# Two layers of recurrent-memory attention and linear attention: the last tile's key-value sum is masked from PSUM, and five of sixteen reciprocal products move from VectorE to GpSimd

## The chip, the cores and the metric

The kernel runs on one core of one Trainium2 chip. A core has five engines that work side by side, each with its own in-order queue: TensorE (PE, with its weight loads PEld), VectorE (DVE), ScalarE (ACT), GpSimd (POOL) and SyncE (SP, which only issues transfers here). The on-chip memory for operands is SBUF; matmul results land in PSUM, of which there are eight banks. The metric is the device time of one execution in microseconds (us); the figure for a kernel is the median of several executions.

## The reference, cut to what matters

Two blocks alternate, A, B, A, B, on a sequence of 2048 tokens of width 512, each with a layernorm in front and a residual sum behind.

Block A is attention with a recurrent memory. The tokens are cut into 64 segments of 32. Eight memory rows are put ahead of each segment, 32 heads of width 128 attend inside it, and the first eight output rows are the memory of the next segment. So segment s+1 can't start before segment s has given its memory.

Block B is linear attention with 32 heads of width 16:

```python
phi = lambda t: jnp.where(t > 0, t + 1, jnp.exp(t)) + 1e-06
kv = jnp.einsum('bhsd,bhse->bhde', pk, v)      # sum over all 2048 tokens
z = jnp.einsum('bhsd->bhd', pk)
num = jnp.einsum('bhqd,bhde->bhqe', pq, kv)
den = jnp.einsum('bhqd,bhd->bhq', pq, z)[..., None] + 1e-06
o = num / den                                   # then o @ wo
```

The sums kv and z run over every token. No output row of B can be made before the last tile of tokens has added its part. Both times that block B runs, this is a point that all work must pass.

## The kernel before, in words

Tokens are handled in 16 tiles of 128 rows. Block A runs as 64 steps, four to a tile. Block B is cut in three. `b_in` takes tile t as soon as block A has finished it: layernorm, keys, values and queries by matmul (lines 1247 and 1281), phi of the keys and queries (`phi`, lines 1231 to 1234), and then the tile's part of kv and z by matmul into two PSUM tiles (lines 1259 and 1265). The parts are added up in SBUF in fp32, `kva` by line 1274 and `za` by line 1276. phi(q) is stored to a scratch in device memory, and so is x.

`b_mid` runs once per block B, after the last tile. Line 1295 masks `kva` to the heads' diagonal blocks and casts it to bf16. Line 1299, four times, makes the matrix `zf_sb` from `za`. Then, for each of four chunks of 128, one matmul (line 1303) multiplies the masked sum with the output weights `MB_sb`, and the product is copied back over the weights. The kernel's helper for copies (`evac`, lines 623 and 624 in the profile) lets the planner choose ScalarE or VectorE.

`b_out` then runs per tile: four matmuls with `zf_sb` give the denominators (line 1353), ScalarE makes their reciprocal as exp(-ln(.)) (lines 1356 and 1358), VectorE multiplies phi(q) by it (line 1359, the reciprocal product), four matmuls with the folded weights give the output rows (line 1361), and VectorE adds them to x (line 1364). In the first block B, `b_out` of tile 0 stands between the two A blocks and the others are spread over the second A block. In the second block B, the sixteen run one behind another at the very end of the kernel ("the last stage"), from data loaded into the space of `Wq_sb`, with the reciprocals in the space of `Wk_sb`, and each result goes out by a store on SP's queue.

The order on each engine is not written by hand. `_Prog.schedule` is a greedy planner that runs when the program is built: it gives every operation a cost (`c_act`, `c_dve`, `c_pe`), keeps a clock for each engine and the eight PSUM banks, and takes the ready operation with the best priority. A priority is the step times 13.5 plus an entry of the table `OFFSET`, found by the stage's name and by the operation's number within that stage; the more negative, the earlier. The whole program, all four blocks, is planned in one go, so each engine's queue is fixed before the run, and what is planned late depends on everything planned before it.

`keep_busy` adds dependency-free matmuls on TensorE, at the lowest priority of their step ("fillers", line 1385). The table `FILL` names the TensorE operation behind which a group of them may start, by stage and number; where that number is not a TensorE operation, the group is left out:

```python
FILL = (("outL", 7, 8), ("resL", 0, 24), ("biL", 5, 4), ("biL", 18, 8), ("biL", 27, 8), ("bm", 7, 21), ("boF", 9, 22),
        ("prepF", 5, 4))
```

Here `biL` is `b_in` of the last tile, `bm` is `b_mid`; the group behind `bm` exists only in the first block B. GpSimd does no arithmetic after the setup: its queue issues transfers of x, phi(q) and of the residual rows (line 639).

Of the kernel before, what the change touches and what calls it, by code (L numbers as in the profile page):

```python
# [9 lines left out]
ALU = mybir.AluOpType  # L10
# [78 lines left out]
    "outL": (-183.35, -223.20, -247.40, -365.15, -74.00, -380.60, -56.90, -223.50, -345.60, -38.20),  # L89
    "resL": (-280.85, -402.40),  # L90
    "biL": (-330.50, -308.55, -333.35, -91.15, -389.95, -228.15, -76.30, -32.45, -294.50, -121.05, -167.60,
        -377.75, -262.40, -270.20, -25.45, -14.60, -313.50, 59.95, -373.25, -319.65, -43.90, -426.45, -404.80,
        159.50, 90.55, -275.05, -114.60, -274.80, -0.20, -245.85, -186.45, -160.00),
    "bm": (-410.80, -480.25, -344.35, -394.70, -170.00, -356.70, -6.85, 40.95, -34.25, 28.70, -27.10, -86.70, 81.00),
    "boF": (-189.35, -384.50, -486.20, -152.40, -345.90, -400.30, -157.90, -333.20, -255.25, -380.60, -218.45),
    "bo": (-354.35, -361.60, -26.00, -195.25, -364.05, -132.50, 137.45, -348.35, -267.60, -258.70, -358.25),
    "ldL": (-68.35, -367.55),
# [5 lines left out]
def c_act(n, ptr=0, sb=0):  # L103
    return 0.17 + 0.833e-3 * n + 0.09 * ptr + 0.04 * sb


def c_dve(n, rate=1):
    return 0.155 + 1.044e-3 * n / rate
# [6 lines left out]
def c_pe(n_mm, n):  # L115
    return n_mm * max(0.0335, (n / 2.4 + 3.0) * 1e-3)
# [390 lines left out]
def _build_kernel(nc, A_x, A_mem0, A_Wq, A_Wk, A_Wv, A_Wo, A_seg_len, B_wqkv, B_wo, out):  # L507
# [7 lines left out]
    NT = S // 128  # L515
# [15 lines left out]
    def sb(name, shape, dt=BF16):  # L531
        return E(nc.sbuf_tensor(name, shape, dt))
# [18 lines left out]
    maskbd_sb = sb("maskbd_sb", [128, 128])  # L551
# [30 lines left out]
    qTl = av(2 * 1024).rearrange("p (r h j x) -> p r h j x", r=2, h=8, j=4)  # L582
    kTl = av(2 * 1024).rearrange("p (r b j g c) -> p r b j g c", r=2, b=2, j=4, g=4)
# [13 lines left out]
    MB_sb = av(4 * D).rearrange("p (c f) -> p c f", c=4)  # L597
    zf_sb = av(4 * 128).rearrange("p (c f) -> p c f", c=4)
    kva = av(512, F32)
    za = av(4, F32)  # L600
# [17 lines left out]
    add = P.add  # L618
# [40 lines left out]
    for i in range(4):  # L659
# [4 lines left out]
        writes=["wqkv"], dsem="dwqkv", after=[P.nodes[-1]], lat=5.0)  # L664
# [38 lines left out]
    for j in range(4):  # L703
# [10 lines left out]
        writes=["selz"])  # L714
# [4 lines left out]
    tl = P.tile()  # L719
    add("pe", lambda t, tl=tl: t.matmul(tl.f32()[:, 0:128], A8_sb[0:8, :], A8_sb[0:8, :], start=True, stop=True), 0.06,  # L720
        reads=XV, tiles=[tl])
    evac(maskbd_sb[:, :], lambda tl=tl: tl.f32()[:, 0:128], 128, tiles=[tl], writes=["maskbd"])
    tl = P.tile()

    def _m0(t, tl=tl):
        for c in range(4):
# [4 lines left out]
         writes=["memT0"])  # L731
# [497 lines left out]
    def phi(tl):  # L1229
# [4 lines left out]
        add("dve", lambda v: v.scalar_tensor_tensor(e_sb, tl.f32()[:, :], 0.0, e_sb, ALU.max, ALU.add), c_dve(512),  # L1234
            reads=["e"], tiles=[tl], writes=["e"])

    def b_in(step, t, last):

        P.at(step, "biL" if t == NT - 1 else "bi")
        tl = layernorm(t)  # L1240
# [13 lines left out]
        kv, z = P.tile(), P.tile()  # L1254
# [12 lines left out]
            return x  # L1267
        add("pe", mz, c_pe(4, 8), reads=["e", "one"], tiles=[z])
        zv = lambda: z.f32()[:, 0:32].rearrange("p (c x) -> p c x", x=8)[:, :, 0]
        if t == 0:  # L1270
            add("dve", lambda v: v.tensor_copy(kva, kv.f32()[:, :]), c_dve(512), tiles=[kv], writes=["kva"])
            add("dve", lambda v: v.tensor_copy(za, zv()), c_dve(4), tiles=[z], writes=["za"])
        else:
            add("dve", lambda v: v.tensor_tensor(kva, kva, kv.f32()[:, :], ALU.add), c_dve(512), reads=["kva"],
                tiles=[kv], writes=["kva"])
            add("dve", lambda v: v.tensor_tensor(za, za, zv(), ALU.add), c_dve(4), reads=["za"], tiles=[z], writes=["za"])
# [11 lines left out]
    def half(v, b):  # L1288
        return v[:, 4 * b:4 * b + 4, :, :].rearrange("p h j x -> p (h j x)")

    def b_mid(step, n):

        P.at(step, "bm")
        km, kk = half(qTl[:, 0], 1), ("qTl", 0, 1)
        add("dve", lambda v: v.tensor_tensor(km.rearrange("p (c x) -> p c x", c=4), kva.rearrange("p (c x) -> p c x", c=4),
                                             maskbd_sb[:, :].unsqueeze(1).to_broadcast([128, 4, 128]), ALU.mult), c_dve(512),
            reads=["kva", "maskbd"], writes=[kk])
        for c in range(4):
            add("dve", lambda v, c=c: v.tensor_scalar_mul(zf_sb[:, c, :], maskbd_sb[:, :], za[:, c:c + 1]), c_dve(128, 2),
                reads=["za", "maskbd"], writes=["zf"])  # L1300
        for c in range(4):
            tl = P.tile()
            add("pe", lambda pe, c=c, tl=tl: pe.matmul(tl.f32()[:, :], km[:, 128 * c:128 * c + 128], MB_sb[:, c, :],
                                                       start=True, stop=True),
                c_pe(1, 512), reads=[kk, ("MB", c)], tiles=[tl])
            evac(MB_sb[:, c, :], lambda tl=tl: tl.f32()[:, :], 512, tiles=[tl], writes=[("MB", c)])


# [22 lines left out]
    def b_out(step, t, last):  # L1331
# [3 lines left out]
        x, xk = x_sb[:, k, :], ("x", k)  # L1335
        e, ek, rb, rk = OWN if t else LEFT
        free = []
        if last:
            rb, rk = RE[:, t, :].bitcast(F32), [("RE", t)]
            free = P.res["Wk"][1]  # L1340
            if t < NT - 1:
                e, ek, x, xk = XE[:, 0, t, :], [("XE", 0, t)], XE[:, 1, t, :], ("XE", 1, t)
            else:
                e, ek = e_sb, ["e"]
# [5 lines left out]
        def md(pe):  # L1350
# [5 lines left out]
        add("act", lambda a: a.activation(rb, td.f32()[:, :], ACTF.Ln, bias=eps6_sb[:, 0:1]), c_act(512, 1),  # L1356
            reads=["eps6"], tiles=[td], writes=rk, after=free)
        add("act", lambda a: a.activation(rb, rb, ACTF.Exp, scale=-1.0), c_act(512, 0, 1), reads=rk, writes=rk)
        add("dve", lambda v: v.tensor_tensor(e, e, rb, ALU.mult), c_dve(512), reads=ek + rk, writes=ek)
        for c in range(4):  # L1360
            add("pe", lambda pe, c=c: pe.matmul(ty.f32()[:, :], e[:, 128 * c:128 * c + 128], MB_sb[:, c, :],
                                                start=(c == 0), stop=(c == 3)),
                c_pe(1, 512), reads=ek + [("MB", i) for i in range(4)], tiles=[ty])
        add("dve", lambda v: v.tensor_tensor(x, x, ty.f32()[:, :], ALU.add), c_dve(512), reads=[xk], writes=[xk],
            tiles=[ty])
# [34 lines left out]
    for t in range(NT):  # L1400
        b_out(2 * NSEG + 2 + t, t, True)
# [44 lines left out]
```

The softmax here doesn't subtract the row's maximum and nothing guards it: scores larger than these inputs give would overflow.

## Time and profile before

| what | value |
|---|---|
| median of 9 executions | 1763.24 us (1759.85 to 1767.76) |
| profiled execution, own time | 1763.24 us |
| its span in the profile | 1761.1 us, granted TensorE clock 0.996 of full speed on average |
| TensorE busy | 1680.3 us, 95% of the span |
| VectorE, ScalarE busy | 1133.5 us and 1130.0 us, 64% each |
| GpSimd busy | 329.1 us, 19% |

The span is what the profiler saw of one execution; the 2.1 us between it and that execution's own time lie around it. Busy shares are means over the whole kernel. The two places that the change touches are short, about 10 us where the first block B turns into the second block A (860 to 871 us of the span) and the last 35 us, and there other engines end the waits than in the long middle. A line of the timeline gives start, length, engine, source line, operation, output and inputs, and in brackets how long the engine stood idle before and for what.

### The profile page before, as it was taken

The page shows a single profiled execution, that of the slowest core. Times are in us where ns is not written, and L with a number is a line of the kernel's source. Part 1 is how long each engine was busy: PE and PEld are TensorE (multiplying, and loading weights), DVE is VectorE, ACT ScalarE, POOL GpSimd, SP SyncE. Part 2 cuts the span into 40 slices and gives each one's busy share as a digit, 9 for nine tenths or more (in the row PEclk, how much of TensorE's full clock was granted, in tenths as well). Part 3 has the DMA queues.
Part 4 walks back from the last instruction along what each step waited for, and adds up shares of the span by engine and source line. Part 5 has one row for each costly group of instructions (what it writes and reads, how often), then busy time and mean ns, then how long its engine had stood idle before and what let it go on. Part 6 is the DMA issues. An engine that isn't in the chain of part 4 may idle for free.

```text
span 1761.1 us, 101223 instructions
## 1 busy us (share of the span) xinstructions
PE 1680.3 (95%) x46099; PEld 1113.8 (63%) x46178; DVE 1133.5 (64%) x3960; ACT 1130.0 (64%) x3069; POOL 329.1 (19%) x660
## 2 busy tenths in 40 slices
PE   5999999999999999999999999999999999999997
PEld 2666666666666666666666666666666666666664
DVE  2566666666666666666566666676666676666656
ACT  3666666666666666666476666666666666666664
POOL 2012211111121112222101221112221112222020
PEclk9999999999999999999999999999999999999999
DMA  9222222222222222222012222222222222223314
GB/s 378 75 37 45 47 44 45 48 43 42 45 46 45 43 51 39 46 48 45 16 32 39 46 48 48 49 40 48 49 43 45 47 42 49 48 45 59 45 32 132
DMA packets 228541, 97.48 MB, mean 55 GB/s; under 512 B 207096, under 2 KB 222256, under 8 KB 226576
## 3 DMA queue, kind: packets, MB, share of 16 engines
q1 hardware_dynamic: 204784, 58.64, 18.3%
q0 software_dynamic: 21744, 19.78, 5.0%
q10 hardware_dynamic: 1584, 12.58, 1.7%
q8 instruction: 361, 5.91, 1.5%
q14 instruction: 68, 0.56, 0.1%
HBM read 29.63 MB, written 10.49 MB: 23 GB/s over the span
## 4 chain that ended last, share of the span: by engine, by line
PE 77%; DMA 10%; ACT 6%; DVE 5%; issue 2%; POOL 1%; ACTq 0%; DVEq 0%
PE pb L794 40%; PE pb L1085 13%; DMA arena_sb<-arena_sb 5%; PE pb L1051 4%; PE pb L816 4%; PE pb L1247 3%; DMA dx_sb<-y_sb 2%; DVE arena_sb L624 2%; PE pb L937 2%; PE pb L1281 2%; ACT arena_sb L623 2%; DMA Wk_sb<-in_A_Wk_dram 1%; PE pb L1110 1%; PE pb L970 1%; PE pb L765 1%
## 5 line engine op out<-in xcount | busy, mean ns | idle before, releaser
L623 ACT ACTIVATE arena_sb<-pb 128x512 bf16<-128x512 f32 (+6 forms) x1375 | 674.6, 509 | 301.0 <-PE pb L794 220.7
L639 POOL DMA_DIRECT2D dx_sb<-y_sb x504 | 256.6, 515 | 1098.3 <-DVE arena_sb L624 484.4
L794 PE MATMUL pb<-Wk_sb,arena_sb 128*32 128x512 bf16 x5120 | 345.7, 381 | 14.9 <-DVE arena_sb L624 6.4
L794 PE MATMUL pb<-Wv_sb,arena_sb 128*32 128x512 bf16 x5120 | 354.8, 379 | 0.7 <-issue 0.7
L794 PE MATMUL pb<-Wq_sb,arena_sb 128*32 128x512 bf16 x5120 | 340.8, 381 | 0.5 <-DMA Wq_sb<-in_A_Wq_dram 0.5
L1085 PE MATMUL pb<-Wo_sb,arena_sb 128*32 128x256 bf16 x10368 | 330.9, 274 | 9.9 <-DVE arena_sb L987 8.7
L1085 PEld LDWEIGHTS pb<-Wo_sb,arena_sb 128*32 128x32 bf16 x10368 | 266.5, 97 | 43.1 <-DVE arena_sb L987 20.2
L624 DVE CAST arena_sb<-pb 128x512 bf16<-128x512 f32 (+3 forms) x459 | 232.5, 519 | 84.4 <-PE pb L794 65.4
L624 DVE COPY arena_sb<-pb 128x512 bf16<-128x512 bf16 (+2 forms) x422 | 150.3, 364 | 166.7 <-PE pb L816 151.7
L624 DVE COPY arena_sb<-arena_sb 32x256 bf16<-32x256 bf16 (+2 forms) x960 | 202.2, 211 | 78.1 <-DMA arena_sb<-arena_sb 18.8
L794 PEld LDWEIGHTS pb<-Wk_sb,arena_sb 128*32 128x32 bf16 x5120 | 131.6, 97 | 119.8 <-DVE arena_sb L624 9.0
L794 PEld LDWEIGHTS pb<-Wq_sb,arena_sb 128*32 128x32 bf16 x5120 | 132.2, 97 | 116.6 <-issue 2.4
L623 ACT ACTIVATE outW_sb<-pb 128x128 fp32r<-128x128 f32 x288 | 79.8, 277 | 159.7 <-PE pb L1085 155.4
L794 PEld LDWEIGHTS pb<-Wv_sb,arena_sb 128*32 128x32 bf16 x5120 | 116.3, 95 | 47.3 <-issue 2.2
L816 PEld LDWEIGHTS pb<-id_sb,arena_sb 128*32 128x32 bf16 x6304 | 110.8, 97 | 53.8 <-DVE arena_sb L624 12.1
L954 ACT ACTIVATE arena_sb<-pb 128x192 bf16<-128x192 f32 (+1 forms) x256 | 81.5, 329 | 93.0 <-PE pb L943 47.8
L816 PE MATMUL pb<-id_sb,arena_sb 128*32 128x128 bf16 x6304 | 136.0, 220 | 0.1
L1121 DVE TENSOR_TENSOR y_sb<-pb,outW_sb 64x256 bf16<-64x256 f32 x158 | 65.8, 417 | 87.7 <-ACT outW_sb L623 85.0
L1051 PE MATMUL pb<-arena_sb 128*128 128x128 bf16 x1024 | 113.9, 220 | 5.4 <-DVE arena_sb L624 4.3
L964 DVE TENSOR_TENSOR arena_sb<-arena_sb 128x128 bf16<-128x128 bf16 x504 | 86.3, 220 | 16.4 <-ACT arena_sb L954 15.4
L1051 PEld LDWEIGHTS pb<-arena_sb 128*128 128x128 bf16 x1024 | 69.4, 97 | 40.9 <-issue 19.6
L987 DVE TENSOR_TENSOR arena_sb<-pb,arena_sb 128x128 bf16<-128x128 f32 x252 | 67.9, 285 | 26.8 <-ACT arena_sb L975 16.2
(125 smaller groups left out, 1976.8 us busy)
## 6 DMA issues: line engine op xcount, KB each, us to landing
arena_sb<-arena_sb SPq DMA_TRANSPOSE x356, 2.9
Wq_sb<-in_A_Wq_dram ACTq DMA_DIRECT2D x1, 4096.0 KB, 13.6
Wk_sb<-in_A_Wk_dram ACTq DMA_DIRECT2D x1, 4096.0 KB, 24.4
Wv_sb<-in_A_Wv_dram ACTq DMA_DIRECT2D x1, 4096.0 KB, 34.9
Wo_sb<-in_A_Wo_dram SPq DMA_DIRECT2D x4, 1024.0 KB, 11.7
xs_scratch<-x_sb POOLq DMA_DIRECT2D x32, 128.0 KB, 2.1
pq_scratch<-arena_sb POOLq DMA_DIRECT2D x32, 128.0 KB, 2.5
dx_sb<-y_sb POOLq DMA_DIRECT2D x252, 12.0 KB, 2.1
```

What stands on the lines that cost most here:

```text
L623: return e.activation(o() if callable(o) else o, i() if callable(i) else i, ACTF.Copy)
L624: return e.tensor_copy(o() if callable(o) else o, i() if callable(i) else i)
L639: add(eng, lambda e: e.dma_start(o, i), 0.55 if eng == "pool" else 0.4, reads=reads, writes=writes, dsem="%s%d" % (kind, k), lat=lat + (0. ...
L794: r = pe.matmul(tl.f32()[32 * j:32 * j + 32, 0:512], blk[:, c, :], W[:, c, o:o + 512], start=(c == 0), stop=(c == 3), tile_position=(0, 32 ...
L816: r = pe.transpose(tt.bf16()[32 * j:32 * j + 32, 128 * i:128 * i + 128], img[:, k, o:o + 32], id_sb[:, :], tile_position=(0, 32 * j))
L954: add("act", lambda a: a.activation(PQ[:, r2, b, 0:nq], tl.f32()[:, 0:nq], ACTF.Exp, scale=SCALE), c_act(nq), tiles=[tl], writes=[("PQ", r ...
L964: add("dve", lambda v, a=a, p_=p_, w_=w_: v.tensor_tensor(wide(Pm[:, k, a, :]), p_.unsqueeze(2).to_broadcast([128, 4, 4, 8]), w_, ALU.mult ...
L987: add("dve", lambda v: v.tensor_tensor(oTb[:, s % NO, 16 * b:16 * b + 16, 0:8], pv.f32()[:, 0:128].rearrange("p (n q) -> p n q", q=8), Rm[ ...
L1051: r = pe.matmul(o, vimg[:, r2, e], Pbx[:, hh, :, :], start=i == 0, stop=False, skip_group_check=True)
L1085: r = pe.matmul(tl.f32()[32 * j:32 * j + 32, 0:256], oT[:, 4 * hh + n, :], Wo_sb[:, 8 * n + hh, 256 * d:256 * d + 256], start=(hh == 0 and ...
L1121: add("dve", lambda v: v.tensor_tensor(y_sb[0:64, k, :], tl.f32()[0:64, 0:256], outW[64:128, w, :].bitcast(F32), ALU.add), c_dve(256), rea ...
L1247: add("pe", lambda pe, c=c: pe.matmul(dst.f32()[:, :], xlnT[:, c, :], wqkv_sb[:, c, o:o + D], start=(c == 0), stop=(c == 3)), c_pe(1, 512) ...
```

## The change

In `b_in` of the last tile, the part of kv is no longer added to `kva`; it stays in its PSUM tile. In `b_mid` there are two masked operands in place of one: the sum of tiles 0 to 14 from SBUF, and the last tile's part straight from PSUM, into a second buffer (the first half of `kTl[:, 1]`). The two are added by the matmul with the output weights, which accumulates two products for each chunk, so there are eight such matmuls in place of four. In the last stage, the reciprocal products of tiles 1, 4, 7, 10 and 13 are issued on GpSimd with a planned cost of 1.3 us.

The table `OFFSET` loses the entry of the removed addition in `biL` and gains entries for the new operations in `bm`. The numbers of the operations in both stages shift by that, and `FILL` is as it was.

```diff
     "biL": (-330.50, -308.55, -333.35, -91.15, -389.95, -228.15, -76.30, -32.45, -294.50, -121.05, -167.60,
-        -377.75, -262.40, -270.20, -25.45, -14.60, -313.50, 59.95, -373.25, -319.65, -43.90, -426.45, -404.80,
-        159.50, 90.55, -275.05, -114.60, -274.80, -0.20, -245.85, -186.45, -160.00),
-    "bm": (-410.80, -480.25, -344.35, -394.70, -170.00, -356.70, -6.85, 40.95, -34.25, 28.70, -27.10, -86.70, 81.00),
+        -377.75, -262.40, -270.20, -25.45, -14.60, -313.50, 59.95, -373.25, -319.65, -43.90, -426.45, 159.50,
+        90.55, -275.05, -114.60, -274.80, -0.20, -245.85, -186.45, -160.00),
+    "bm": (-450.00, -415.80, -480.25, -344.35, -394.70, -170.00, -356.70, -356.70, -6.85, 40.95, 40.95, -34.25,
+        28.70, 28.70, -27.10, -86.70, -86.70, 81.00),
...
+    kv_last = [None]
...
-        if t == 0:
+        if t == NT - 1:
+            kv_last[0] = kv
+            add("dve", lambda v: v.tensor_tensor(za, za, zv(), ALU.add), c_dve(4), reads=["za"], tiles=[z], writes=["za"])
+        elif t == 0:
...
-        km, kk = half(qTl[:, 0], 1), ("qTl", 0, 1)
-        add("dve", lambda v: v.tensor_tensor(km.rearrange("p (c x) -> p c x", c=4), kva.rearrange("p (c x) -> p c x", c=4),
-                                             maskbd_sb[:, :].unsqueeze(1).to_broadcast([128, 4, 128]), ALU.mult), c_dve(512),
-            reads=["kva", "maskbd"], writes=[kk])
+        masked = lambda v: v.rearrange("p (c x) -> p c x", c=4)
+        kv = kv_last[0]
+        parts = ((half(qTl[:, 0], 1), ("qTl", 0, 1), lambda: kva, ["kva"], []),
+                 (kTl[:, 1, 0].rearrange("p j g c -> p (j g c)"), ("kTl", 1, 0), lambda: kv.f32()[:, :], [], [kv]))
+        for km, kk, v_, rd, tls in parts:
+            add("dve", lambda v, km=km, v_=v_: v.tensor_tensor(
+                masked(km), masked(v_()), maskbd_sb[:, :].unsqueeze(1).to_broadcast([128, 4, 128]), ALU.mult), c_dve(512),
+                reads=rd + ["maskbd"], tiles=tls, writes=[kk])
...
-            add("pe", lambda pe, c=c, tl=tl: pe.matmul(tl.f32()[:, :], km[:, 128 * c:128 * c + 128], MB_sb[:, c, :],
-                                                       start=True, stop=True),
-                c_pe(1, 512), reads=[kk, ("MB", c)], tiles=[tl])
+            for i, (km, kk, *_) in enumerate(parts):
+                add("pe", lambda pe, c=c, tl=tl, i=i, km=km: pe.matmul(tl.f32()[:, :], km[:, 128 * c:128 * c + 128], MB_sb[:, c, :],
+                                                                       start=i == 0, stop=i == 1),
+                    c_pe(1, 512), reads=[kk, ("MB", c)], tiles=[tl])
...
-        add("dve", lambda v: v.tensor_tensor(e, e, rb, ALU.mult), c_dve(512), reads=ek + rk, writes=ek)
+        if last and t % 3 == 1:
+            add("pool", lambda g: g.tensor_tensor(e, e, rb, ALU.mult), 1.3, reads=ek + rk, writes=ek)
+        else:
+            add("dve", lambda v: v.tensor_tensor(e, e, rb, ALU.mult), c_dve(512), reads=ek + rk, writes=ek)
```

## The prediction, made before the changed kernel was run

> **What bounds the kernel now.** First the page: busy shares, then the chain that ended last.
>
> ```profile
> PE 1680.3 (95%) x46099; PEld 1113.8 (63%) x46178; DVE 1133.5 (64%) x3960; ACT 1130.0 (64%) x3069; POOL 329.1 (19%) x660
> ...
> PE 77%; DMA 10%; ACT 6%; DVE 5%; issue 2%; POOL 1%; ACTq 0%; DVEq 0%
> ```
>
> TensorE bounds the kernel as a whole, and none of its work in block A is touched. A gain can only come from the short places where another engine ends the waits. So next the timeline of the turn from the first block B to the second block A:
>
> ```profile
> 865.29 0.68 DVE L1274 TENSOR_TENSOR arena_sb<-arena_sb,pb 128x512 f32<-128x512 f32 x1
> ...
> 865.86 1.04 PE L1385 MATMUL pb<-Wv_sb,id_sb 128*128 128x256 bf16 x8
> ...
> 866.05 0.68 DVE L1295 TENSOR_TENSOR arena_sb<-arena_sb,maskbd_sb 128x512 bf16<-128x512 f32 x1
> 866.06 0.60 ACT L1231 ACTIVATE arena_sb<-pb 128x512 bf16<-128x512 f32 x1 [1.67 <-PE pb L1281]
> ...
> 866.79 0.60 PE L1303 MATMUL pb<-arena_sb 128*128 128x512 bf16 x2
> ...
> 867.22 1.08 ACT L623 ACTIVATE arena_sb<-pb 128x512 bf16<-128x512 f32 x2 [0.56 <-PE pb L1303]
> ```
>
> Addition, mask, first product with the weights, copy: a chain on VectorE, TensorE, ScalarE. TensorE fills its wait with eight fillers; ScalarE stands 0.56 us. The second block B has the same picture: addition 1734.18, mask 1734.94, product 1735.68, copy 1736.11.
>
> Last, the end of the kernel, as busy time by stretches (PE, PEld, DVE, ACT, POOL, each with its count; clock; DMA) and as timeline:
>
> ```profile
> 1744.00:1748.00 4.00, 4.00 (x31) 2.18 (x30) 4.00 (x8) 4.00 (x9) 0.00 (x0) 1.00 0.36 123
> 1748.00:1752.00 4.00, 3.84 (x22) 1.56 (x21) 4.00 (x8) 4.00 (x9) 0.00 (x0) 1.00 0.32 107
> 1752.00:1756.00 4.00, 3.35 (x14) 1.04 (x14) 4.00 (x8) 2.73 (x6) 0.00 (x0) 1.00 0.30 100
> ```
>
> ```profile
> 1752.75 0.68 DVE L1359 TENSOR_TENSOR Wq_sb<-Wq_sb,Wk_sb 128x512 bf16<-128x512 bf16 x1
> 1753.35 0.68 DVE L1364 TENSOR_TENSOR Wq_sb<-Wq_sb,pb 128x512 bf16<-128x512 bf16 x1
> 1753.47 1.26 ACT L1358 ACTIVATE Wk_sb<-Wk_sb 128x512 f32<-128x512 f32 x2
> ...
> 1757.09 1.04 PE L1361 MATMUL pb<-arena_sb 128*128 128x512 bf16 x4 [0.16 <-DVE arena_sb L1359]
> 1758.16 0.69 DVE L1364 TENSOR_TENSOR x_sb<-x_sb,pb 128x512 bf16<-128x512 bf16 x1
> ```
>
> VectorE is full and ends last; ScalarE is full until 1754.73 and close behind; GpSimd is empty. Products and additions start 0.60 us apart.
>
> **The change, part by part**, against the profiled execution: own time 1763.24 us, the median too; span 1761.1.
>
> *Addition out of the chain.* Once the last tile's kv is in PSUM, the mask can start where the addition stood, at 865.29. The fp32 row of line 1274 reads PSUM at 0.68 us, the mask's row is 0.68, so the new mask is taken at 0.68. It ends 0.76 us earlier, at 865.97. The product can start at 866.03, where TensorE, without the eight fillers (next paragraph), is just past the queries' matmuls. But each chunk needs two products: 0.22 us more (four of line 1361 take 0.87) before the copy. So the copy may start at 867.22 - 0.76 + 0.22 = 866.68, behind phi's exponential, which ends at 866.66. Gain 0.54 us, at each block B. VectorE is relieved too, so `zf_sb` and phi(q) are no later; the weights' copies of line 624 ended at 869.06, ahead of the first output product at 870.32. The other six matmuls (1.3 us) have room there: TensorE runs 2.3 us of fillers.
>
> *Mask of tiles 0 to 14.* 0.68 us more on VectorE, at the highest priority, ready when tile 14's addition ends (830.70 and 1692.21). At 830.61 the softmax product of line 1026 is queued behind, then the copies that feed line 1051. TensorE has 3.5 us of key and query matmuls there, ScalarE its copies: cost 0, with 0 to 0.6 us as ends. If that cover goes, the next segment's value products are late.
>
> *Fillers.* The list of `b_in` shrinks by one, so number 27 is the exponential of phi(q), no TensorE operation: eight fillers vanish in both blocks, 0.87 us each, at 865.86 and 1734.75. Nothing waits for them. Number 7 of `b_mid` is now the second product of the first chunk, so 21 fillers may start earlier. They ended at 870.34, just where the output product started; TensorE has 1.3 us of products more and 0.87 us of fillers less to do before. If the planner keeps all 21 ahead of the output product, the first gain of 0.54 is lost; ends 0 and 0.54, taken at 0, since the planner issues fillers singly and prefers the product once ready. The granted clock is 0.50 from 1728 to 1732 in the last block and 1.00 from 1736; the dropped fillers lie after the rise, and matmuls follow at once.
>
> *Five products on GpSimd.* VectorE's 32 operations at 0.60 us become 27, so 3.0 us less. ScalarE now sets the floor: its last exponential, 0.54 us earlier, ends at 1754.19; then 0.06 to the product, 0.68, 1.13 to the addition (from 1757.03 to 1758.16) and 0.69, so 1756.75 against 1758.85 now. Of these 2.10 us, 0.54 are the earlier start and 1.56 belong to GpSimd's help. What a product lasts on GpSimd isn't in the trace. The nearest rows:
>
> ```profile
> L678 POOL TENSOR_SCALAR_AFFINE_SELECT arena_sb<-arena_sb 128x160 bf16<-128x160 bf16 x2 | 0.9, 468 | 0.1
> ...
> L678 POOL TENSOR_SCALAR_AFFINE_SELECT id_sb<-id_sb 128x128 bf16<-128x128 bf16 x1 | 0.3, 317 | 0.1
> ```
>
> From 32 columns (214 ns, setup) to 128 (317) it is 1.1 ns an element, from 128 (406) to 160 (468) 1.9. For 512 columns that makes 0.74 to 1.15 us with one operand, and 1.83 us if a second operand doubles the steeper slope. I take 1.2. One comes every three tiles, 3.3 us, so the queue holds; its only transfer there, the store of phi(q) at 1737.05, is ahead of all five. A late product stalls TensorE in order, with tiles behind it: tile 13's, from about 1752.0, ends at 1753.3, and TensorE needs 0.87 us each for tiles 13 and 14 before 15's starts at 1755.0. So it just fits; at 1.83 it costs some 0.5 us.
>
> Unknown is also what GpSimd's arithmetic does to VectorE; no row shows both at work. Let w be VectorE's loss per moved product. Help is the smaller of 1.56 and 5 x (0.60 - w). Low end w = 0: VectorE's rows keep their 0.68 us while GpSimd issues transfers. High end: VectorE stands through it, 1.83. I take 0.4, near the low end because only issues were seen beside it: help 1.0 us, ends +1.56 and -6.2.
>
> Here the Trainium skill speaks against the change: "SBUF — State Buffer", section "SBUF: two separate sides", says that a VectorE operation with two SBUF inputs and a GpSimd operation that reads SBUF exclude each other for a whole instruction. Line 1359 has two such inputs, line 1364 only one. "GPSIMD Engine Reference", section 3.1, states about 2.6 cycles an element at 1.2 GHz, an estimated 1.1 us here; VectorE blocked for all of it gives 5 x (0.60 - 1.1), a loss of 2.5 us in place of the gain of 1.0. No row of this trace shows the lock.
>
> *The second A block is planned anew.* Everything behind tile 14's addition in the first block B is planned from other clocks and banks, 900 us of it. How uneven that stretch is, GpSimd's stores of x show, four steps apart:
>
> ```profile
> 1104.16 0.56 POOL L639 DMA_DIRECT2D xs_scratch<-x_sb  x1 [1.88 <-DVE x_sb L1162]
> 1155.44 0.56 POOL L639 DMA_DIRECT2D xs_scratch<-x_sb  x1 [1.88 <-DVE x_sb L1162]
> ...
> 1471.46 0.56 POOL L639 DMA_DIRECT2D xs_scratch<-x_sb  x1 [1.92 <-DVE x_sb L1162]
> 1525.42 0.56 POOL L639 DMA_DIRECT2D xs_scratch<-x_sb  x1 [2.86 <-DVE x_sb L1162]
> ```
>
> The like work takes 51.28 us and 53.96 us. The fourteen distances from 949.58 to 1683.53 have a mean of 52.43 and a scatter of 0.97, so 3.6 us over fourteen; part of it is the spread of executions. All at the best (51.24) would be 16.6 us less, all at the worst 21.4 more. I take 0 with a scatter of 3 to 4 us.
>
> Sum: 0.54 + 0.54 + 1.0 = 2.1 us less, 1761.1.
>
> **The rivals.** *The second A block comes out shorter.* For it: its groups lie 16.6 us above their best, those of the first block A only about 9 (best 50.60). Against: one transfer wait decides a group, and priorities are the same. One scatter: 1761.1 - 3.6 = 1757.5.
>
> *It comes out longer.* The same scatter, 1764.7 at one and 1768.3 at two; slower by 0.2% from +5.7 us on. Against it: a group is bounded by TensorE whatever the order.
>
> *GpSimd holds up VectorE in the last stage* (the other side, one mechanism): both read SBUF, and each product makes VectorE wait. Above w = 0.60 the help is negative, at 0.82 the whole gain is gone, and at 1.52 the kernel is 0.2% slower; at 1.83, 1763.24 - 1.08 + 6.2 = 1768.3. For it: VectorE has no gap there. Against: three of the five VectorE operations that go with each GpSimd product are additions with a PSUM input, which may run beside it.
>
> *The front gains don't arrive*: fillers hold the first output product, and ScalarE's queue the second. Then only the help is left, 1762.2.
>
> **How the numbers follow.** 0.2% of 1763.24 is 3.5 us, about what a measurement of this kernel can tell from no change. Forecast, with lost front gains: 0.46, between 1759.7 and 1766.8. Shorter second block: 0.31, faster. Longer second block: 0.15, and GpSimd's hold: 0.08, both slower. So faster 0.31, same 0.46, slower 0.23. The likeliest case's own range is 1759.7 to 1765. The 8-in-10 range cuts off one scatter and a half below, 1755.8, and above half of the slower cases, at 1767.8.
>
> **What the profile after would show.** Right: fillers 135 in place of 151; sixteen weight loads for the folded weights in place of eight; no fp32 addition between the kv matmul and the mask, and ScalarE's copies about 0.5 us closer behind the kv matmuls; in the last stage VectorE with gaps, ScalarE without, and some 17.5 us from its first logarithm to the last exponential. Wrong: VectorE's products 1 us long or behind waits for GpSimd; product to product on GpSimd over 3.3 us; TensorE waiting for GpSimd; fillers up to the output product. The forecast would fail most likely in the distances between the stores of x, should their sum from first to last move by more than 4 us.

## The result, and the profile after

The changed kernel takes 1769.19 us (median of 11 executions, 1764.95 to 1774.98) against 1762.43 us for the kernel before (33 executions on the same chip, 1758.42 to 1767.76). The ratio is 1.004, with a 95% interval of [1.003, 1.005]: slower by 0.4%, some 7 us, where the prediction had 2.1 us less. The profiled execution of the changed kernel has an own time of 1774.61 us, at the upper end of its executions, and a span of 1772.8 us. All lines of the changed kernel are numbered differently: products of the weights 1314 (before 1303), denominators 1364 (1353), reciprocals 1367 and 1369 (1356 and 1358), the products on VectorE 1373 and on GpSimd 1371 (1359), output product 1375 (1361), addition to x 1378 (1364), fillers 1399 (1385).

The page's busy times and its chain that ended last:

```profile
PE 1680.8 (95%) x46091; PEld 1112.9 (63%) x46170; DVE 1129.4 (64%) x3950; ACT 1131.5 (64%) x3074; POOL 335.4 (19%) x665
...
PE 76%; DMA 11%; ACT 5%; DVE 5%; issue 2%; POOL 1%; ACTq 0%; DVEq 0%
```

Busy times are those of before within 6.3 us; VectorE's fell, TensorE's rose by 0.5 us. Nothing here says where 7 us went: the work is nearly the same. The timeline of the first turn (after the first block B):

```profile
871.32 0.68 DVE L1305 TENSOR_TENSOR arena_sb<-pb,maskbd_sb 128x512 bf16<-128x512 f32 x1
...
872.09 0.60 ACT L1232 ACTIVATE arena_sb<-pb 128x512 bf16<-128x512 f32 x1 [1.67 <-PE pb L1287]
872.58 1.08 ACT L624 ACTIVATE arena_sb<-pb 128x512 bf16<-128x512 f32 x2
...
873.54 0.70 ACT L1367 ACTIVATE arena_sb<-pb,eps_sb 128x512 f32<-128x512 f32 x1
873.90 2.46 PE L1399 MATMUL pb<-Wv_sb,id_sb 128*128 128x256 bf16 x21
...
874.11 0.62 ACT L624 ACTIVATE arena_sb<-pb 128x512 bf16<-128x512 f32 x1
874.59 0.65 ACT L1369 ACTIVATE arena_sb<-arena_sb 128x512 f32<-128x512 f32 x1
...
876.19 1.03 PE L1375 MATMUL pb<-arena_sb 128*128 128x512 bf16 x4
```

The mask reads PSUM (`pb`) in 0.68 us, and ScalarE's copies of the weights follow the exponential (872.09) without the idle 0.56 us of before. But a third copy now stands on ScalarE, between logarithm (873.54) and exponential (874.59), and the 21 fillers end at 876.36, beside the output product at 876.19.

The end of the kernel, from the same view:

```profile
1746.50 1.03 PE L1314 MATMUL pb<-arena_sb 128*128 128x512 bf16 x4
1747.41 1.29 PE L1364 MATMUL pb<-Wq_sb,arena_sb 128*128 128x128 bf16 x20
1748.98 0.81 PE L1314 MATMUL pb<-arena_sb 128*128 128x512 bf16 x3
1749.61 0.69 DVE L625 CAST arena_sb<-pb 128x512 bf16<-128x512 f32 x1 [1.26 <-PE pb L1314]
1750.55 1.37 POOL L1371 TENSOR_TENSOR Wq_sb<-Wq_sb,Wk_sb 128x512 bf16<-128x512 bf16 x1 [1.35 <-ACT Wk_sb L1369]
1751.56 0.61 PE L1375 MATMUL pb<-arena_sb,Wq_sb 128*128 128x512 bf16 x2 [1.32 <-DVE arena_sb L625]
...
1763.69 1.23 POOL L1371 TENSOR_TENSOR Wq_sb<-Wq_sb,Wk_sb 128x512 bf16<-128x512 bf16 x1 [1.54 <-ACT Wk_sb L1369]
1769.12 0.33 SPq L640 DMA_DIRECT2D out_dram<-x_sb  x1
```

The products of the third and fourth chunk (1748.98) stand behind 24 denominator matmuls (20 in the row at 1747.41), so VectorE waits 1.26 us for a copy. The last GpSimd product starts at 1763.69 and the last store is issued at 1769.12, yet the span ends at 1772.8, that is 3.71 us later; before, it was 2.19 us (1758.88 to 1761.1). In between GpSimd runs the drain (DRAIN) that closes its program: it starts at 1763.65, takes 8.95 us and ends at 1772.60, while SP's own drain ends at 1771.09. The same drain stands in the trace of before, far ahead of the end (the rows of GpSimd's drain before and after: its length in ns, its start):

```profile
L1405 POOLq DRAIN  x1: 8239/8239/8239, 1737.0 to 1737.0; - x1
...
L1419 POOLq DRAIN  x1: 8946/8946/8946, 1763.7 to 1763.7; - x1
```

Before, GpSimd's last operation is the transfer of phi(q) at 1737.05, which it ends at 1737.60, and the drain ends 7.67 us later, at 1745.27. After, its last operation is the last product, which ends at 1764.92, and the drain ends 7.68 us later. In all sixteen profiles of this case it is 7.67 to 7.69 us, with and without products.

### The profile page after: what moved, and what is told of

The parts are those of the page before. It is cut to its first block, busy times and chain, and to the rows that moved or that the text cites. A ratio compares the mean times of both kernels' runs of the same rounds, so it can differ in the third digit from the quotient of the medians.

```text
span 1772.8 us, 101207 instructions
## 1 busy us (share of the span) xinstructions
PE 1680.8 (95%) x46091; PEld 1112.9 (63%) x46170; DVE 1129.4 (64%) x3950; ACT 1131.5 (64%) x3074; POOL 335.4 (19%) x665
## 4 chain that ended last, share of the span: by engine, by line
PE 76%; DMA 11%; ACT 5%; DVE 5%; issue 2%; POOL 1%; ACTq 0%; DVEq 0%
PE pb L795 39%; PE pb L1086 13%; DMA arena_sb<-arena_sb 6%; PE pb L1052 4%; PE pb L817 4%; PE pb L1250 3%; DMA dx_sb<-y_sb 2%; ACT arena_sb L624 2%; DVE arena_sb L625 2%; PE pb L938 2%; PE pb L1287 2%; DMA Wk_sb<-in_A_Wk_dram 1%; PE pb L971 1%; PE pb L1111 1%; PE pb L766 1%
```

## Where the time went

The 32 stores of x by GpSimd (0 to 15 in the first layer, 16 to 31 in the second) and the last stores cut the span into the same pieces in every kernel. Two pieces repeat to 0.03 us wherever the instructions in them are the same: from the last z matmul of a block B (line 1265 of before) to VectorE's addition to x of tile 0 at the first turn, and to the issue of the last store at the second.

| piece (us) | before | after |
|---|---|---|
| first A block, store 0 to 14 | 717.64 | 722.24 |
| first turn: z matmul to addition to x | 6.76 | 6.59 |
| second A block, store 16 to 30 | 733.96 | 738.99 |
| store 30 to 31 (last segments of the layer) | 42.37 | 43.09 |
| last z matmul to last store | 25.34 | 23.83 |
| last store to end of span | 2.19 | 3.71 |

The first A block is the same program up to 836 us in all kernels here (but for the banks' numbers in two of them) and lasts 717.6 to 722.2 us in 16 profiled executions, so its 4.6 us are the spread of executions. The last stage gained 1.51 us, and the drain took 1.52 us back. The first turn gained 0.17 us. What is left, 5.0 us and 0.7 us, lies in the second A block and in store 30 to 31. The table compares one execution of each kernel, and that of the changed kernel is 5.4 us above its median; means over several kernels follow below.

The instructions of the second A block stand in the same order as before; only the numbers of the PSUM banks are exchanged (1 for 7, 2 for 1, and so on). Apart from the two turns and the last stage, another order was written in steps 61 to 63 of each layer alone. There the mask of the first fifteen tiles stands on VectorE between two operations of the softmax:

```profile
836.40 0.42 DVE L1027 TENSOR_TENSOR arena_sb<-arena_sb 128x256 bf16<-128x256 bf16 x1
836.74 0.69 DVE L1305 TENSOR_TENSOR arena_sb<-arena_sb,maskbd_sb 128x512 bf16<-128x512 f32 x1
837.34 0.22 DVE L1028 TENSOR_TENSOR arena_sb<-arena_sb 128x64 bf16<-128x64 bf16 x1
```

The planner answers by giving small copies to ScalarE and by taking value products ahead of the sums on TensorE. In the first layer, from the start of this softmax product to the last z matmul, it costs 0.24 us (34.35 us, before 34.11). In the second layer transfers wait in the same stretch, and the spread from execution to execution hides a cost of this size.

## The experiments

Each ratio is to the kernel before on the same chip. "The early mask" is the mask of tiles 0 to 14, "the late mask" that of the last tile's sum, from PSUM.

**One part alone.** e1 is the changed kernel without GpSimd's products:

```diff
-        if last and t % 3 == 1:
-            add("pool", lambda g: g.tensor_tensor(e, e, rb, ALU.mult), 1.3, reads=ek + rk, writes=ek)
-        else:
-            add("dve", lambda v: v.tensor_tensor(e, e, rb, ALU.mult), c_dve(512), reads=ek + rk, writes=ek)
+        add("dve", lambda v: v.tensor_tensor(e, e, rb, ALU.mult), c_dve(512), reads=ek + rk, writes=ek)
```

e2 is the kernel before with these products alone, the same lines the other way round.

> The last tile's kv masked from PSUM and added in the matmul, no products on GpSimd. Theory A, the loss comes with the mask and the matmul part (its eight missing fillers, the moved mask, the new order of some thirty operations around step 62): the kernel stays 6 to 7 us above before, the two long blocks A are longer. Theory B, the loss comes with GpSimd's arithmetic: 0.5 to 1.1 us below before, since both chains are 0.54 us shorter. Theory C, any change of the program moves the two long blocks by some us, without a cause in its own work: anything from 4 below to 8 above before, and the first A block, whose order is the same up to 836 us, would be longer too.

> Only the five products on GpSimd; all before the last stage is in the order of before. Theory A: 1 us below to 1.5 above before (the last store up to 1.5 us earlier, GpSimd's closing drain up to 1.5 us later than SP's end). Theory B: 6 us above before. Theory C: the long blocks move by some us though nothing in them was changed.

Measured: e1 1.0037 [1.0021, 1.0053], 1769.55 against 1761.17 us; e2 1.0006 [0.9994, 1.0018]. So the loss comes with the masks and the new turn; GpSimd's part alone makes no loss that can be told from none. The pieces show why the parts do not add: from the last z matmul to the last store the kernel before takes 25.34 us, e2 24.94, e1 25.75 and the changed kernel 23.83. The products help by 0.40 us with the old turn and by 1.92 with the new one; the new turn alone loses 0.41. In e1 VectorE waits 1.26 us for a chunk's product too (from 1743.06 to 1744.32) and still has nearly all of its 32 operations ahead; with five of them on GpSimd the later start no longer sets the end. A second part of the difference may be that with the old turn VectorE's products start while GpSimd's run. From the timeline of e2:

```profile
1739.58 1.17 POOL L1360 TENSOR_TENSOR Wq_sb<-Wq_sb,Wk_sb 128x512 bf16<-128x512 bf16 x1 [2.70 <-ACT Wk_sb L1358]
...
1740.05 1.24 DVE L1362 TENSOR_TENSOR Wq_sb<-Wq_sb,Wk_sb 128x512 bf16<-128x512 bf16 x1
```

VectorE's product takes 1.24 us in place of 0.68, and a second one (at 1746.75, GpSimd's from 1746.16 to 1747.32) 1.12; together 1.0 us that VectorE loses over the five moved products, 0.2 for each.

**The vanished fillers.** The list of `b_in` is one shorter, so the filler group of eight behind number 27 is left out. The kernel before, without that group:

```diff
-    FILL = (..., ("biL", 18, 8), ("biL", 27, 8), ("bm", 7, 21), ...
+    FILL = (..., ("biL", 18, 8), ("bm", 7, 21), ...
```

> Only the two groups of eight fillers behind the last query matmuls are left out; every other instruction is in the order of before, on every engine. Theory A, with the fillers as its part: some us above before, the second block A or the last stage at the lower clock. Theory B: as before within 1 us. Theory C: may lie some us off, in the long blocks.

Measured: 1.0006 [0.9994, 1.0018]. So the vanished fillers don't make the loss: at most 3 us of it are left for them.

**The drain.** The changed kernel with four products on GpSimd, the last for tile 10:

```diff
-        if last and t % 3 == 1:
+        if last and t % 3 == 1 and t < 12:
```

> The changed kernel with tile 13's product back on VectorE, so the last product on GpSimd is tile 10's, some 2.7 us earlier. If GpSimd's closing drain (8.95 us in the profile after, ending at 1772.60 where SP had ended at 1771.09) ends the kernel, its end comes no more than 0.4 us behind SP's, and the kernel is about 1.2 us faster than the changed one. If the drain is not what ended it: no change. Either way some 5 to 6 us above before remain under theories A and C.

Measured: 1.0039 [1.0027, 1.0051]. From the last store to the end of the span it takes 2.18 us again, and z matmul to last store 24.08 us: 0.25 lost, 1.53 won back, 1.28 us together. That is 0.0007, and the ratio did not show it beside the rest; the drain is settled by the profiles alone: in e2, whose last product ends 4.6 us ahead of the last store, the span also ends 1.1 us later (3.28 us after the last store), and in every kernel whose GpSimd ends earlier than that it is 2.2.

**The early mask held back.** e1, with the early mask made to read two names that the last step writes, so that it runs at that step's end; steps 61 to 63 then have the order of before. e6 has four GpSimd products as well:

```diff
-        parts = ((half(qTl[:, 0], 1), ("qTl", 0, 1), lambda: kva, ["kva"], []),
+        parts = ((half(qTl[:, 0], 1), ("qTl", 0, 1), lambda: kva, ["kva", ("oTx", 0, 0), ("oTx", 0, 1)], []),
```

> As e1 (last tile's kv masked from PSUM, no products on GpSimd), but the mask of tiles 0 to 14 also waits for the copies of the last segment's attention, so it runs at the end of the last step and no longer in step 62; steps 61 to 63 are then in the order of before. Theory D, the early mask in step 62 made the loss (it takes VectorE ahead of the softmax and pushes four copies to ScalarE, so the last memory rows and the last residual rows come about 1 us later, and in the last block those rows then queue behind more of the big loads): the distance between the last two stores of x falls from 44 to about 42 us, and the kernel lies 0 to 2 us below before. Theory E, the loss is made behind the last step, by eight products in place of four and the mask from PSUM: 5 to 8 us above before, as e1.

> As e5, with the products of tiles 1, 4, 7 and 10 on GpSimd, so that its closing drain is hidden. Theory D: 1 to 4 us below before, 1760.5 at most by the before of these runs, and the fastest of all. Theory E: 4 to 7 us above before, as e4.

Measured: e5 1.0014 [1.0001, 1.0027], e6 1.0011 [1.0000, 1.0021]. Most of the loss is gone once the order of steps 61 to 63 is left alone; e6's interval lies wholly below e4's, [1.0027, 1.0051], from which it differs in the place of the mask alone (and in the chip). But neither theory gave the range: both kernels still lie 2 to 2.5 us above before, where theory D had them below. The second A block took 728.34 and 729.69 us, store 30 to 31 took 41.12 and 41.18.

**The early mask alone.** The kernel before with one more mask of `kva` at the early place, whose result nobody uses (the old mask stays); steps 61 to 63 get e1's order:

```diff
+        if t == NT - 1:
+            P.at(step, "dm")
+            add("dve", lambda v: v.tensor_tensor(..., kva..., maskbd..., ALU.mult), c_dve(512),
+                reads=["kva", "maskbd"], writes=[("qTl", 0, 1)])
```

> The kernel before, with one more masking of the sum of tiles 0 to 14 at the place where the changed kernel has it, its result overwritten later; step 61 to 63 are then in the order of e1 on every engine, all else is in the order of before. Theory D: 5 to 8 us above before, the distance between the last two stores of x 43 to 44 us in place of 42. Theory E: 0 to 1 us above before.

Measured: 1.0005 [0.9996, 1.0014]. That the reordered steps cost the 7 us by themselves, as theory D had it, is excluded: at most 2.5 us of it. Store 30 to 31 does take 44.86 us in e7's profile, longer than theory D said, but that is the slowest of e7's twelve executions. The turn alone has 0.0014 (e5), the early mask alone 0.0005, both together 0.0037 to 0.0047 in five kernels; that the two make more than their sum is likely, but at the upper ends of their intervals the two alone would reach 0.0041.

**The banks.** Left over as a difference of the whole second A block were the bank numbers. The kernel before with the changed kernel's numbers (e8), e1 with those of before (e9), and on the same chip the changed kernel again (e10). The line is that of e9; e8 has the list (0, 7, 1, 2, 5, 3, 6, 4):

```diff
-    P = _Prog(nc, banks)
+    P = _Prog(nc, [banks[j] for j in (0, 2, 3, 5, 7, 4, 6, 1)])
```

> The kernel before with the eight PSUM banks renamed throughout, so that its second block A uses, tile by tile, the banks that the changed kernel uses there; order and waits are those of before. Theory F, the banks' numbers make the second block A slower in the changed kernel (3 to 5 us between its first and last store of x): this kernel lies 3 to 6 us above before, perhaps with a longer first block A too. Theory G, the numbers are without effect: within 1.5 us of before.

> As e1, with the banks renamed throughout so that the second block A uses those of the kernel before. Theory F: 1 to 3 us above before, from the last steps alone. Theory G: as the changed kernel on this chip, 5 to 7 us above before.

> The changed kernel beside e8 and e9, on the same chip, since the time of before moved by 4 us between the earlier groups of runs. If the loss is a matter of the program: 5 to 8 us above before again. If it is one of the chip: it may shrink to the 1 to 2 us of e5 to e7.

Measured: e8 1.0004 [0.9996, 1.0013], e9 1.0047 [1.0035, 1.0059], e10 1.0039 [1.0027, 1.0052]. The numbers of the banks have no effect that can be measured, and the loss of the changed kernel repeats.

**Half-clock windows.** Over the profiled executions of these kernels, the five with early mask and new turn (after, e1, e4, e9, e10) need 735.7 us on average for the second A block (734.05 to 738.99), the seven others (before, e2, e3, e5 to e8) 730.1 us (727.67 to 733.96). What the five have in the records is TensorE at half clock for stretches of 3.41 us. Busy time by stretches of e1, cut at the borders of these stretches (length, then busy time and count of PE, PEld, DVE, ACT, POOL; granted clock; DMA share; GB/s):

```profile
1360.66:1364.07 3.41, 1.32 (x32) 0.93 (x34) 0.83 (x3) 1.75 (x7) 3.41 (x8) 1.00 0.19 45
1364.07:1367.49 3.42, 3.42 (x65) 2.39 (x58) 2.35 (x8) 1.18 (x4) 0.43 (x1) 0.50 0.02 4
1527.91:1531.32 3.41, 1.32 (x73) 0.60 (x64) 2.04 (x6) 0.80 (x4) 0.56 (x1) 1.00 0.13 43
1531.32:1534.74 3.42, 3.42 (x59) 2.58 (x42) 2.47 (x9) 2.31 (x9) 0.55 (x1) 0.50 0.17 43
```

The same second place in e5:

```profile
1521.94:1525.35 3.41, 1.67 (x65) 0.82 (x62) 2.85 (x11) 1.29 (x5) 0.56 (x1) 1.00 0.11 38
1525.35:1528.77 3.42, 3.42 (x73) 2.84 (x77) 3.03 (x14) 3.23 (x12) 0.55 (x1) 1.00 0.16 43
```

TensorE stands in e1 at 1361 for phi(q), which went out to memory and comes back (1.87 us; no wait in e5), and in both kernels near 1529 behind the residual rows, which come by transfer (2.09 us in e1, 1.74 in e5). Where it worked only 1.32 us of a stretch, the next is granted 0.50; in e5, with 1.67, it keeps 1.00. At the second place it worked 1.09 to 1.50 us in the five kernels, and four of them got a half clock behind it; 1.67 to 2.04 us in the other seven, and none did. At the first place four of the five got one, and two of the seven. (In the profile of the changed kernel one lies at 1055 instead.) If that is the cause, work for TensorE in the two waits must bring the time back. e1, and as a control the kernel before, with twelve fillers put into TensorE's queue ahead of each of the two waiting products:

```diff
+    for key in ((100, "bo", 2), (113, "mem0", 0)):
+        i, = [i for i, n in enumerate(P.committed) if n.key == key]
...
+                for _ in range(12):
+                    y = pe.matmul(tl.f32()[:, 0:256], id_sb[:, :], Wv_sb[:, 0, 0:256], start=True, stop=True)
...
+            P.committed.insert(i, nd)
```

> The same kernel as e1_psum_only (mask from PSUM, no GpSimd products; all other instructions in the same order), with twelve filler matmuls of 256 columns (0.109 us each, 1.3 us) put into TensorE's queue ahead of the two places of the second A block where TensorE stood and a half-clock window followed: the b_out product of line 1364 at 1362.58 of e1 (gap 1.87 us) and the left product of line 944 at 1530.60 (gap 2.09 us). Theory 'half-clock windows': TensorE's busy time in the two windows of 3.41 us rises from 1.1-1.5 to 2.4-2.8 us, no window at half clock follows, the stretch from store 16 to store 30 of x falls from 735.8 to 730-732 us, and the ratio from e1's 1.0037 to 1.000-1.002. Rival 'the stalls themselves': the granted clock is a side show; the stretch stays at 734-737 and the ratio at 1.003-1.005, or more, if the fillers end after the data have come.

> The kernel before with the same twelve fillers ahead of the same two products: the control. Theory 'half-clock windows': the kernel before had one such window in two of its seven like profiles, near 1361, so the mean gains about 0.5 us and the ratio is 0.999-1.0005. Rival 'the fillers save time of another kind': this kernel gains as much as the one with the changed turn, 4 us, ratio 0.9975. Should the fillers end late and cost time, the ratio is 1.0005-1.0015 here and the same amount must be taken off the other run.

Measured: e11 1.0016 [1.0003, 1.0029], e12 0.9994 [0.9985, 1.0004]. The same stretches of e11, first and second place:

```profile
1364.37:1367.78 3.41, 2.61 (x46) 1.89 (x48) 0.81 (x3) 1.73 (x7) 3.41 (x8) 1.00 0.18 45
...
1531.62:1535.04 3.42, 3.42 (x88) 2.35 (x86) 3.17 (x13) 2.14 (x8) 1.11 (x2) 1.00 0.12 43
```

TensorE is busy for 2.61 and 3.42 us there, no half clock comes in the whole second A block, and e1's 0.0037 fell to 0.0016, so by 0.0021 or 3.7 us. The control fell by 0.0006; with that taken off, 0.0015 or 2.6 us are left. The intervals of e1 and e11 overlap, so the size is rough, but e11's ends at 1.0029 and the five kernels with early mask and new turn lie at 1.0037 to 1.0047. The second A block of e11's profile took 733.30 us (730.92 in e12's), not the 730 to 732 expected.

The profiles show one execution of each kernel; the record has the mean granted clock of every execution. It is 0.9952, 0.9957, 0.9952 and 0.9957 on average in e1, e4, e9 and e10, where before has 0.9972 and 0.9971 on the same two chips; 0.9960 in the changed kernel's first runs; 0.9965 to 0.9973 in e2, e3 and e5 to e8; 0.9967 in e11 (before 0.9971) and 0.9979 in e12. So the low clock comes with early mask and new turn over all executions, not in the profiled ones alone, and the fillers take it away: the theory holds in kind. The clock lost is 0.0014 to 0.0020 of the span, 2.5 to 3.5 us if TensorE were busy all through it (an estimate from these clocks), of a loss of 6.5 to 8.3 us: at most a third to a half. The rest of the loss isn't clock.

**What remains of the new turn.** Last, two kernels with these fillers and four GpSimd products each, which differ in the turn alone: the old one (e13), and the new one with the early mask held back as in e5 (e14):

> The kernel before (old turn) with the twelve fillers of e12 at the two stalls and four products of the last stage on GpSimd (tiles 1, 4, 7, 10; the closing drain of GpSimd is then over before the last store). Theory 'GpSimd's help is real and only the drain took it back': 0.6 us of e12 and 1.0 us of the last stage add up, ratio 0.9985-0.9995. Rival 'the products bring nothing': ratio as e12, 0.999-1.0005.

> The kernel of e6 (mask from PSUM; the mask of the first fifteen tiles held back to the end of its step, so that the order of steps 61 to 63 stays; four GpSimd products) with the same twelve fillers: e13 and this one differ by the turn alone. Theory 'the turn gains little': 0.2-0.5 us at the first turn, 0 at the second; ratio to the kernel before 0.0001-0.0003 below that of e13. Rival 'the turn's other form loses time by itself', as e5's 1.0014 would have it: ratio 0.001-0.0015 above that of e13.

Measured: e13 1.0000 [0.9989, 1.0011], e14 1.0000 [0.9990, 1.0011]. e13 lies where its rival 'the products bring nothing' had it, and its profile agrees: from the last z matmul to the last store four products gain 0.14 us with the old turn (25.20 us, before 25.34). The new turn neither gains nor loses what can be measured, once the steps before it keep their order and TensorE doesn't idle in the two waits. The profiles have the exact part: z matmul to addition to x 6.59 us in place of 6.76 at the first turn, and z matmul to last store 24.07 us in place of 25.20. These 1.3 us (0.0007) are within the interval. No version here beats the kernel before by more than the noise.

**What stays open.** Why TensorE's waits at 1361 and 1529 hit the clock more often with early mask and new turn: the order of instructions there is the same. At 1529 the wait is 2.10 us on average in the five profiles and 1.77 in the seven others; at 1361 it is 1.40 to 1.87 us in the five, 1.52 to 1.87 in four of the others and none in three. But single executions overlap: e3 and e6, without that combination, wait 2.27 and 2.21 us at 1529, and no half clock follows, with 1.85 us of work in e3's emptier stretch and 1.68 in e6's: how the wait falls to the borders of the stretches counts too, and not its length alone. The residual rows landed 3.08 to 3.31 us after their issue in e1 and e10, 2.63 to 2.72 in e5 and e8, but 3.18 and 3.19 in e3 and e6; what the slower transfers met is not in the records. That they meet other transfers at another moment, since the second A block begins at another time, is a guess. Of e11's 0.0016 (2.8 us) about half is found: 1.1 us in store 30 to 31 (42.27 us, 41.15 in e12) and 0.2 in the two turns (0.41 lost, 0.17 gained). e5's 0.0014 isn't found in any piece of its profile, and e14 against e13 doesn't show it.

## Why the prediction was wrong, by its own steps

The prediction's sum was 2.1 us less; measured was some 7 us more. The steps that failed are the two terms put at 0, "Mask of tiles 0 to 14" and "The second A block is planned anew": in their place the profiles show 1.8 us more in store 30 to 31 and 5.6 us more in the second A block, on average. At most a third to a half of that is TensorE at half clock; for the rest the cause stays open. A smaller step failed besides: the sum ended at the last store, and GpSimd's drain behind it took 1.52 us.

*"Addition out of the chain", 0.54 us at each block B.* Right where it was reckoned, lost a few instructions later. From the z matmul to the first logarithm of the last stage it takes 2.86 us in place of 3.54, a gain of 0.68. At the first turn the logarithm gains the same 0.68 (1.45 us behind phi's exponential, before 2.13), the reciprocal product 0.33, the output product 0.16, the addition to x 0.17. What failed is the sentence that the weights' copies "ended at 869.06, ahead of the first output product at 870.32", taken to stay so: the planner put three of the four copies on ScalarE, where there were two, and the third (0.62 us, at 874.11) stands ahead of the exponential. The other 0.17 went to the 21 fillers, which the working had named as an end and set to 0. So at the first turn the rival "The front gains don't arrive" came true. At the second turn the other six matmuls, said to "have room there", were put behind 24 denominator matmuls, VectorE's copy waited 1.26 us for them, and e1, which has the turn without GpSimd's products, ends 0.41 us later than before.

*"Mask of tiles 0 to 14", cost 0.* This failed. The queue's cover was argued engine by engine, for an order that was taken to stay; the planner answered the mask of 0.69 us with another order on three engines. Store 30 to 31 took 43.3 us on average in the five kernels with early mask and new turn and 41.6 in six others (before, e2, e3, e5, e6, e8), so 1.8 us more; in e7, with the early mask alone, it took 44.86. With this mask held back, most of the whole loss went (1.0014 and 1.0011).

*"The second A block is planned anew", 0 with a scatter of 3 to 4 us.* The premise failed: the order there is unchanged. Yet the time did change there, by waits and clock, 5.6 us to the longer side on average. The rival "It comes out longer" named the place, the sign and a size (5.7 us and more) that came, with a cause that didn't, so its hit is luck. The scatter of groups of four steps, read as chance of the order, comes mainly from the same steps each time: the two distances shown, 51.28 and 53.96 us, are 51.32 and 54.60 in the changed kernel, and 51.2 to 52.0 and 53.7 to 54.9 in all sixteen profiles. That transfers are what waits there is argued, not shown for each group.

*"Fillers", cost 0.* Right: e3 gives 1.0006 with 1 in its interval, and the count fell by 16, as stated.

*"Five products on GpSimd", help 1.0 us.* The duration was right: 1.17 to 1.37 us, taken at 1.2. The sum of head start and help in the last stage, 0.54 + 1.0, was 1.54 us, measured 1.51; but the parts are -0.41 for the turn and +1.92 for the help, so the agreement is luck. The floor that ScalarE sets was right: 17.66 us from its first logarithm to its last exponential, forecast 17.5. What failed is the end: the sum ended at the last store, and the drain behind it wasn't in it, +1.52 us. The trace of before had its price: the working names "the store of phi(q) at 1737.05" as GpSimd's last work there, and the drain ends 7.67 us behind it. So, with the turn's loss counted, the last stage gains nothing with five products and 1.26 us with four; with the old turn the help is 0.40 and 0.14.

*The rival "GpSimd holds up VectorE".* Its mechanism is there, but it was too small to matter in the changed kernel. The Trainium skill, "SBUF — State Buffer", section "SBUF: two separate sides", has VectorE operations with two SBUF inputs and GpSimd operations that read SBUF exclude each other for a whole instruction. The two kinds hardly met here, since the planner put additions with a PSUM input beside GpSimd's products; these kept 0.68 to 0.69 us. Where they met, the traces agree with the page: of VectorE's products one took 0.90 us in place of 0.68 (at 1761.80, GpSimd's from 1760.98 to 1762.15), in e2 two took 1.24 and 1.12, and all three end 0.55 us after GpSimd's product, though they start 0.35 to 0.69 us ahead of its end. GpSimd's that start inside one of VectorE's took 1.37, 1.25 and 1.23 us, the two others 1.17, and the three end 1.02 us after VectorE's. So all but some 0.13 to 0.15 us of the later one waits for the end of the earlier (0.68 - 0.55 and 1.17 - 1.02). So VectorE's loss w for each moved product was 0.04 us in the changed kernel and 0.2 in e2, where the prediction took 0.4. The 1.1 us estimated from "GPSIMD Engine Reference", section 3.1, agrees with these 1.17.

## What to carry to other kernels

An instruction with free time on its own engine isn't free when a planner writes the order: compare the orders of the two programs, engine by engine, before costing it at nothing, and look for where a relieved engine's work went. A kernel bounded by TensorE that waits at fixed places for transfers may sit just above the point where the clock falls; a few tenths of a microsecond of wait can then cost up to 1.7 more, and fillers ahead of the waiting product bring them back. Work moved to GpSimd near the end must be over some 5.5 us ahead of the last store (an estimate for this kernel: the drain's 7.7 us less the 2.2 us that the end takes anyway).

## What was not expected of the hardware

- GpSimd's closing drain ended 7.68 us after the last product's end (1763.69 + 1.23 to 1772.60), and 7.67 us after the end of its last transfer where it had no products (before). Behind four products (e4) it is the same; as the last product then ended 7.2 us ahead of the last store in place of 4.2, it was hidden.
- The granted clock falls to 0.50 for 3.41 us behind a stretch of 3.41 us in which TensorE did work, but little. In the second A blocks of these profiles it fell each time with up to 1.38 us of work, never with 1.85 or more, and between these it did either (fell after 1.76 in e9, not after 1.50 in e4). In a stretch at half clock up to 1.7 us of work are lost (half of 3.41).
- A product of VectorE with two SBUF inputs that starts inside one of GpSimd's ends 0.55 us after GpSimd's end, for starts 0.35 to 0.69 us ahead of that end: it takes 0.90 us here and 1.24 and 1.12 in e2, alone 0.68. An addition with a PSUM input beside it keeps its 0.68 to 0.69.
- Exchanged numbers of PSUM banks, the same in all else, made no difference: 1.0004 [0.9996, 1.0013].
